# Grouped-query decode attention on one core: matmul addresses by bit masks, a three-pass y-sum for the last head, and an earlier row sum

## The chip, the cores and the metric

The kernel runs on one core of one Trainium2 chip. The metric is the device time of one execution in microseconds (us), taken in several runs on the same chip and given as a median. A profile of one execution gives busy times, waits and the records of single instructions and DMA packets; its span is about 2 us shorter than the device time. An execution counts as slow when it is over 1.5% above the fastest of its kernel; only fast ones are compared here, and where a kernel ran once its state is unknown. PE is the matrix engine, PEld its weight loads, PEq its sequencer, DVE the vector engine, ACT the scalar engine, POOL the general-purpose engine and SP the engine that issues the loads.

## The reference

One query token attends to 65536 keys. There are 32 query heads and 8 key/value heads, so four query heads share one head of K and V.

```python
B, Hq, Hkv, Sq, Sk, D = 1, 32, 8, 1, 65536, 128      # q, k, v: bf16
k = jnp.repeat(k, Hq // Hkv, axis=1)
v = jnp.repeat(v, Hq // Hkv, axis=1)
scores = jnp.einsum("bhqd,bhkd->bhqk", q, k) * D ** -0.5
out = jnp.einsum("bhqk,bhkd->bhqd", softmax(scores), v)
```

K and V are 134 MB each. Every byte is used once, for four heads.

## The kernel before

A head's keys are handled in two halves of 32768; each half fills a buffer of 128 partitions x 256 slots x 128 values (8 MB). There are two buffers for K and one for V. All loads go out from one queue in a fixed order, and each waits until PE is done with what stood in its buffer:

```python
def load_k(g, b):
    SP.wait((s_sc, 16 * g - 8 + 8 * b if g else 0))      # scores of the earlier head are done
    ...
def load_v(g, b):
    done = 2 * (2 * g + b)
    if (g, b) == (G - 1, 1):          # the last V load goes in eight pieces
        SP.wait((s_vc, done - 1))     # first half of the V buffer is free
        load(v, g, b, 0, s_v[0], CUTS[0], CUTS[1])
        SP.wait((s_vc, done))         # all of it is free
        ...
        for lo, hi, s in list(zip(CUTS, CUTS[1:], s_v))[1:]:
            load(v, g, b, 0, s, lo, hi)
    ... # two halves for the two V loads before that, else one load after s_vc >= done
# CUTS = [0, 128, 192, 224, 232, 240, 248, 252, 256], in slots
```

DVE transposes K in place, 64 or 128 slots at a time. PE then makes the scores. A half of K takes eight turns of a loop ("parts") of eight matmuls each; the addresses come from two counters, x (the tile) and n (the part):

```python
with block("pe_part"):
    nc.regs_alu(r_n, r_n, 1, op=ALU.add)
    ...                                     # x and n are the values of r_x and r_n
    r_k = (x % 2) * (SL * D) + (n // 2) * (PS * D) + (n % 2) * (2 * D) + SL * D
    r_w = (n % 4) * (-8) + 28
    r_o = (x % 2) * 1024 + (n // 4) * 512
    take(s_kt, 1)                           # wait for the transpose, count it down
    for u in range(2):
        for s in range(2):
            for e in range(2):
                i = pe.matmul(out=..r_o.., lhsT=..r_w.., rhs=..r_k.., ...)
    i.then_inc(s_sc, 1)
    nc.br_cmp(r_n, 7, "pe_part", "pe_skip", "IS_LT", engines=only)
```

The values of a half take 64 matmuls of 512 columns ("wide"), into four groups y of PSUM columns. Two spare matmuls in their middle write to a place that nobody reads for their value. After each head DVE multiplies by a selector and sums over the four y:

```python
def collect():
    n = DV.mark(dve.tensor_tensor(out=vy[:, :, :], in0=vacc,          # vy: [P, 4, D], fp32
        in1=sely[:, :, None].to_broadcast([P, 4, D]), op=ALU.mult))
    DV.after(n)
    return DV.mark(dve.tensor_reduce(out=vs[:, 0:D],
        in_=vy[:, :, :].rearrange("p y d -> p d y"), axis=AX.X, op=ALU.add))
```

For the last 24 slots, which arrive in small pieces, there are single narrow matmuls, with the row sum of the softmax among them. The last "gather" adds the y-sums; ACT scales, and a small store ends the program:

```python
for t in range(SL - TAIL, SL):
    if t == CUTS[5]:                        # slot 240
        pe.matmul(out=pl, lhsT=sel[:, :], rhs=vs[:, ...], start=True, stop=True).then_inc(s_pe, 1)
    if t in CUTS:
        pe.wait_ge(s_v[CUTS.index(t)], 16)  # this piece of V has landed
    pe.matmul(out=fin, lhsT=et[...], rhs=io[:, t, :], ...)
pe.wait_ge(s_dv, collected[G - 1])          # the y-sums are there
gather(D, start=False, stop=True).then_inc(s_pe, 1)
```

Of the kernel before, what the change touches and what calls it, by code (L numbers as in the profile page):

```python
# [8 lines left out]
ALU = mybir.AluOpType  # L9
ACT = mybir.ActivationFunctionType  # L10
AX = mybir.AxisListType
PE = mybir.EngineType.PE

P = 128
D = 128
SL = 256
KEYS = P * SL
G = 8
H = 4
WB = 160  # L20
PS = 64
TAIL = 24
CUTS = [0, 128, 192, 224, 232, 240, 248, 252, 256]
# [24 lines left out]
def kernel(  # L48
# [7 lines left out]
    nc = tc.nc  # L56
    SCALE = float(D) ** -0.5
    fp32 = mybir.dt.float32
# [5 lines left out]
    def sb(name, shape, dt):  # L64
        return ctx.enter_context(nc.sbuf_tensor(name, shape, dt))

    def ps(name, shape):
        return ctx.enter_context(nc.psum_tensor(name, shape, fp32))

    def sem(name):  # L70
        return ctx.enter_context(nc.semaphore(name))
# [7 lines left out]
    sel = sb("sel", [P, H], fp32)  # L79
    selq = sb("selq", [P, 16], fp32)  # L80
    sely = sb("sely", [P, 4], fp32)
# [5 lines left out]
    ex = sb("ex", [P, 4, 512], bf16)  # L87
    et = sb("et", [P, 2, 512], bf16)
    vs = sb("vs", [P, D + 2], fp32)
    vy = sb("vy", [P, 4, D], fp32)  # L90
    fall = sb("fall", [H, G - 1, D + 2], fp32)
    r7 = sb("r7", [H, G - 1], fp32)
    o = sb("o", [H, D], bf16)
# [2 lines left out]
    sc, vacc = acc[:, 0:2048], acc[:, 2048:2560].rearrange("p (y d) -> p y d", d=D)  # L96
    pt = ps("pt", [P, 512])
    pb = ps("pb", [P, 512])
    pf = ps("pf", [P, 512])
    pl, fin = pb[0:H, 8:9], pf[0:H, 0:D]  # L100
# [7 lines left out]
    s_sc, s_pe, s_vb, s_vc = sem("s_sc"), sem("s_pe"), sem("s_vb"), sem("s_vc")  # L108
# [11 lines left out]
    sp, act, dve, gp, pe = nc.sync, nc.scalar, nc.vector, nc.gpsimd, nc.tensor  # L120
    SP = Queue(nc, sp, None)
    ACTQ = Queue(nc, act, s_ac)
    DV = Queue(nc, dve, s_dv)
# [48 lines left out]
    for g in range(1, G):  # L172
# [11 lines left out]
    n = GP.mark(gp.memset(ident[:, :], 0.0))  # L184
    GP.after(n)
    p_ident = GP.mark(gp.affine_select(
        out=ident[:, :], in_=ident[:, :], compare_op=ALU.not_equal, fill=1.0, base=0,
        pattern=[[-1, P]], channel_multiplier=1,
    ))
    n = DV.mark(dve.memset(acc[:, :], 0.0))  # L190
    collected = {-2: n, -1: n}
# [3 lines left out]
        out=sel[:, :], in_=ident[:, :].rearrange("p (x h) -> p h x", h=H), axis=AX.X, op=ALU.add  # L195
    ))
    n = DV.mark(dve.tensor_reduce(
        out=selq[:, :], in_=ident[:, :].rearrange("p (x r) -> p r x", r=16), axis=AX.X, op=ALU.add
    ))
    DV.after(n)  # L200
    DV.mark(dve.tensor_reduce(
        out=sely[:, :], in_=selq[:, :].rearrange("p (y h) -> p y h", h=H), axis=AX.X, op=ALU.add
    ))
    DV.wait((s_q, 16))
    for a in range(4):
        d_qT = DV.mark(dve.transpose(
            out=qT[32 * a:32 * a + 32, :, :].rearrange("p s n -> p (s n)"),
            in_=q_in[:, :].bitcast(u32),
# [61 lines left out]
            in_=ex[:, 2 * b:2 * b + 2, :].rearrange("p i n -> p (i n)"),  # L270
        ).then_inc(s_et, 1)

    def collect():
        n = DV.mark(dve.tensor_tensor(  # L274
            out=vy[:, :, :], in0=vacc, in1=sely[:, :, None].to_broadcast([P, 4, D]), op=ALU.mult
        ))
        DV.after(n)
        return DV.mark(dve.tensor_reduce(  # L278
            out=vs[:, 0:D], in_=vy[:, :, :].rearrange("p y d -> p d y"), axis=AX.X, op=ALU.add
        ))  # L280

    def keep(g):
# [3 lines left out]
    for g in range(G):  # L286
        for _ in transposes(g, 0):
            pass
        for i, _ in enumerate(transposes(g, 1)):
            if i == 0 and g:  # L290
                DV.wait((s_vc, 4 * g - 2))
                weights(g - 1, 1)
        top(g)
        softmax(g)
        if 0 < g < G - 1:

            weights(g, 0)
            DV.wait((s_vc, 4 * g))
            collected[g - 1] = collect()
            ACTQ.wait((s_dv, collected[g - 1]))  # L300
            clear(g)
        elif g:
            DV.wait((s_vc, 4 * g))
            DV.after(collect())
            collected[g - 1] = DV.mark(dve.memset(vacc, 0.0))
            weights(g, 0)
        else:
            weights(g, 0)
        if g:
            n_kept = keep(g - 1)  # L310
# [4 lines left out]
    for i in range(2):  # L315
        n = DV.mark(dve.reciprocal(out=r7[:, i::2], in_=fall[:, i::2, D + i]))
    DV.after(n)
    n = DV.mark(dve.tensor_tensor(
        out=o7, in0=fall[:, :, 0:D], in1=r7[:, :, None].to_broadcast([H, G - 1, D]),
        op=ALU.mult,  # L320
    ))
    SP.wait((s_dv, n))
    sp.dma_start(
        out=out[0, 0:(G - 1) * H, 0, :].rearrange("(g h) d -> h g d", h=H), in_=o7
    ).then_inc(s_st, 16)
    DV.wait((s_vb, 2 * G))
    collected[G - 1] = collect()
    DV.wait((s_pe, 3 * G + 2))
    d_rl = DV.mark(dve.reciprocal(out=rl[:, :], in_=pl))
    ACTQ.wait((s_dv, d_rl), (s_pe, 3 * G + 3))  # L330
    n = ACTQ.mark(act.activation(out=o[:, :], in_=fin, func=ACT.Copy, scale=rl[:, :]))  # L331
# [5 lines left out]
    for g in range(G):  # L337
# [5 lines left out]
        for a in range(4):  # L343
            r = slice(32 * a, 32 * a + 32)
            c0 = 28 + 32 * a
            if a == 3:
# [4 lines left out]
                out=wz[r, :, c0:c0 + H].rearrange("p (s w) h -> p s w h", s=2),  # L351
                in_=qTb[r, :, :, g, :],
# [5 lines left out]
    def take(s, n):  # L358
        down(pe, PE, s, n, wait=True)
# [8 lines left out]
    def wide(ch, tt):  # L368
        c, w0 = tt % 4, tt * 32 + 16 * (ch % 2)
        return pe.matmul(  # L370
            out=vacc[32 * c:32 * c + 16, :, :],
            lhsT=et[:, ch // 2, w0:w0 + 16],
            rhs=io[:, PS * ch + 4 * tt:PS * ch + 4 * tt + 4, :],
            start=False, stop=False, skip_group_check=True,
        )

    only = OrderedEngineSet([PE])
    r_x, r_n = (nc.alloc_registers(r, engines=only) for r in ("x", "n"))

    def block(name):  # L380
        return nc.body(name, valid_engines=only)


    nc.regs_mov(r_x, -1)
    nc.br("pe_head", engines=only)
    with block("pe_head"):
        take(s_w, 4)
# [1 line left out]
        nc.br("pe_tile", engines=only)  # L389
    with block("pe_tile"):  # L390
        nc.regs_alu(r_x, r_x, 1, op=ALU.add)
        nc.regs_mov(r_n, -1)
        nc.br_cmp(r_x, 2 * G, "pe_part", "pe_skip", "IS_LT", engines=only)
    with block("pe_part"):
        nc.regs_alu(r_n, r_n, 1, op=ALU.add)
        x = nc.snap(r_x, engines=only, donate=True, min_val=0, max_val=2 * G + 1)
        n = nc.snap(r_n, engines=only, donate=True, min_val=0, max_val=7)
        r_k = (x % 2) * (SL * D) + (n // 2) * (PS * D) + (n % 2) * (2 * D) + SL * D
        r_w = (n % 4) * (-8) + 28
        r_o = (x % 2) * 1024 + (n // 4) * 512  # L400
        take(s_kt, 1)
        for u in range(2):
            for s in range(2):
                for e in range(2):
                    i = pe.matmul(  # L405
                        out=bass.AP(acc, r_o, [[2560, P], [1, 512]]),
                        lhsT=bass.AP(wz, r_w + ((2 * s + e) * WB - 4 * u), [[4 * WB, P], [1, P]]),
                        rhs=bass.AP(
                            io, r_k + (u * D + 64 * s + e), [[IO, P], [4 * D, 16], [2, 32]]
                        ),  # L410
                        start=False, stop=False, skip_group_check=True,
                    )
        i.then_inc(s_sc, 1)
        nc.br_cmp(r_n, 7, "pe_part", "pe_skip", "IS_LT", engines=only)
    with block("pe_skip"):
        nc.br_cmp(r_x, 2, "pe_next", "pe_values", "IS_LT", engines=only)
    with block("pe_values"):
        take(s_et, 1)
        for ch in range(4):
            if ch == 3:  # L420
                pe.wait_ge(s_v[2], 16)
            elif ch != 1:
                take(s_v[ch // 2], 16)
            for tt in range(16 if ch < 3 else (SL - TAIL) % PS // 4):
                if (ch, tt) == (3, 8):
                    pe.wait_ge(s_v[3], 16)
                i = wide(ch, tt)
            if ch == 1:
                i.then_inc(s_vc, 1)

                for _ in range(2):
                    pe.matmul(  # L432
                        out=pt[0:16, :], lhsT=et[:, 0, 0:16], rhs=et[:, 0, :],
                        start=True, stop=True,
                    )
        i.then_inc(s_vb, 1)
        nc.br_cmp(r_x, 2 * G + 1, "pe_rest", "pe_tail", "IS_LT", engines=only)
    with block("pe_rest"):
# [2 lines left out]
        i.then_inc(s_vc, 1)  # L441
        nc.br("pe_next", engines=only)
    with block("pe_next"):
        nc.regs_alu(r_n, r_x, 2, op=ALU.mod)
        nc.br_cmp(r_n, 0, "pe_tile", "pe_softmax", "IS_EQ", engines=only)
    with block("pe_softmax"):
        take(s_mg, 1)
# [3 lines left out]
            out=pb[:, 0:1], in_=nrow[:, :, :].rearrange("o x h -> o (x h)"), identity=ident[0:1, 0:1]  # L451
        ).then_inc(s_pe, 1)
        nc.br("pe_head", engines=only)
    nc.switch_bb("pe_tail")

    for t in range(SL - TAIL, SL):
        if t == CUTS[5]:
            pe.matmul(  # L458
                out=pl, lhsT=sel[:, :], rhs=vs[:, D + (G - 1) % 2:D + (G - 1) % 2 + 1],
                start=True, stop=True,  # L460
            ).then_inc(s_pe, 1)
        if t in CUTS:
            pe.wait_ge(s_v[CUTS.index(t)], 16)
        w0 = t % PS // 4 * 32 + 16 + 4 * (t % 4)
        pe.matmul(  # L465
            out=fin, lhsT=et[:, 1, w0:w0 + H], rhs=io[:, t, :], start=(t == SL - TAIL), stop=False,
            skip_group_check=True,
        )
# [32 lines left out]
```

## Time and profile before

| what | value | view |
|---|---|---|
| device time | 630.08 us, median of 3 (629.99 to 630.28) | runs |
| packets of the load queue | 99.1% of 16 DMA engines' span | queue table |
| PE, DVE, ACT busy | 56%, 54%, 6% | busy table |
| one part of the scores | 2.52 us, of which PE idles 0.6 us | timeline |
| last V piece landed to last gather | 0.30 us | semaphore records, timeline |

From the profile page of the kernel before, first the busy time of the engines (us, share of the span, number of instructions), then DMA by fortieths of the span (9 is 90% or more busy), then the load queue (packets, MB, share of 16 engines' span).

```profile
PE 352.5 (56%) x2136; PEld 138.0 (22%) x2136; DVE 339.2 (54%) x131; ACT 36.1 (6%) x32; POOL 7.5 (1%) x40
...
DMA  8999999999999999999999999999999999999996
...
q1 hardware_dynamic: 6656, 268.45, 99.1%
```

The load queue is the only thing that is busy all the time. No engine with arithmetic passes 56%.

From the groups of the same page (line, engine, operation, tiles out and in, number; then busy us and mean ns of one; then the idle time ahead of them and what ended it):

```profile
L405 PE MATMUL acc<-io,wz 128*128 x1024 | 270.7, 416 | 179.7 <-issue 92.2
L227 DVE STREAM_TRANSPOSE io<-io 128x4096 uint32<-128x4096 uint32 (+1 forms) x54 | 279.0, 5207 | 161.2 <-DMA io<-in_k_dram 161.2
...
L274 DVE TENSOR_TENSOR vy<-acc,sely 128x512 f32<-128x512 f32 x8 | 5.3, 660 | 11.9 <-PE acc L370 11.9
...
L278 DVE TENSOR_REDUCE vs<-vy 128x128 f32<-128x512 f32 x8 | 8.2, 1021 | 0.3
```

The score matmuls (L405) had 179.7 us of idle PE ahead of them, of which 92.2 us are labelled "issue": nothing that the profile shows was waited for. That label suggests register arithmetic, and the change aims at it. The timeline of PE in a K stage (start, duration, then in brackets the idle time ahead) shows it turn by turn:

```profile
44.98 1.91 PE L405 MATMUL acc<-io,wz 128*128 x8 [0.60 <-issue]
47.50 1.92 PE L405 MATMUL acc<-io,wz 128*128 x8 [0.61 <-issue]
50.07 1.92 PE L405 MATMUL acc<-io,wz 128*128 x8 [0.65 <-issue]
```

The timeline of the tail of the kernel before:

```profile
622.03 1.06 PE L370 MATMUL acc<-io,et 128*16 128x512 bf16 x10 [1.36 <-DMA io<-in_v_dram]
...
623.14 0.69 DVE L274 TENSOR_TENSOR vy<-acc,sely 128x512 f32<-128x512 f32 x1 [11.94 <-PE acc L370]
623.38 0.42 PEld L465 LDWEIGHTS pf<-io,et 128*4 128x4 bf16 x8 [0.59 <-DMA io<-in_v_dram]
...
623.83 0.19 PE L458 MATMUL pb<-vs,sel 128*4 128x1 f32 x2
623.86 1.03 DVE L278 TENSOR_REDUCE vs<-vy 128x128 f32<-128x512 f32 x1
624.04 0.87 PEld L465 LDWEIGHTS pf<-io,et 128*4 128x4 bf16 x16
...
624.95 0.09 PEld L364 LDWEIGHTS pf<-vs,sel 128*4 128x4 f32 x2
...
625.43 0.36 ACT L331 ACTIVATE o<-pf,rl 4x128 bf16<-4x128 f32 x1 [31.86 <-PE pf L364]
```

L465 are the single slots, L458 is the row sum, L278 the reduction, L364 the last gather. The pieces of V for slots 232, 240, 248 and 252 landed (last of 16 DMA engines, from the trace's semaphore records) at 623.34, 624.00, 624.34 and 624.65.

### The profile page before, as it was taken

The numbers are of one execution on the slowest core, as the hardware profiler recorded it, in microseconds if no ns is written. First come the engines' busy times: TensorE is split into PE (matmuls) and PEld (weight loads), VectorE is DVE, ScalarE is ACT, GpSimd is POOL, SyncE is SP. The second block draws the span as 40 slices with busy tenths as digits, with TensorE's granted clock in tenths as the row PEclk, the third lists the DMA queues.
The fourth block names the chain that finished last, engine by engine and source line by source line (L and its number), as shares of the span: only waits on it lengthen the run. The fifth ranks groups of instructions, "written<-read, shape, count | busy, mean of one in ns | idle before, by whom it ended". The sixth has DMA issues, their size and how long they took to land. (4 is left out here: it accounts for less than half of the span.)

```text
span 628.0 us, 6627 instructions
## 1 busy us (share of the span) xinstructions
PE 352.5 (56%) x2136; PEld 138.0 (22%) x2136; DVE 339.2 (54%) x131; ACT 36.1 (6%) x32; POOL 7.5 (1%) x40
## 2 busy tenths in 40 slices
PE   0676483834838348382573816748176581887335
PEld 0222131311313113130231302213022230332112
DVE  3984835649065490655807558085570846684211
ACT  0000200020000200002000020000200002000100
POOL 1000000000000000000000000000000000000000
PEclk9999596975969759596696966969669595899677
DMA  8999999999999999999999999999999999999996
GB/s 368 434 459 409 459 409 459 409 451 417 451 417 451 417 443 426 442 426 434 434 430 438 422 447 417 451 405 463 401 463 405 463 405 463 399 434 434 434 432 277
DMA packets 6715, 268.48 MB, mean 428 GB/s; under 512 B 825, under 2 KB 1081, under 8 KB 1465
## 3 DMA queue, kind: packets, MB, share of 16 engines
q1 hardware_dynamic: 6656, 268.45, 99.1%
q8 instruction: 1, 0.02, 0.0%
q10 hardware_dynamic: 56, 0.01, 0.0%
q14 instruction: 2, 0.01, 0.0%
HBM read 268.44 MB, written 0.01 MB: 427 GB/s over the span
## 5 line engine op out<-in xcount | busy, mean ns | idle before, releaser
L405 PE MATMUL acc<-io,wz 128*128 x1024 | 270.7, 416 | 179.7 <-issue 92.2
L227 DVE STREAM_TRANSPOSE io<-io 128x4096 uint32<-128x4096 uint32 (+1 forms) x54 | 279.0, 5207 | 161.2 <-DMA io<-in_k_dram 161.2
L405 PEld LDWEIGHTS acc<-io,wz 128*128 x1024 | 105.5, 103 | 345.0 <-issue 267.4
L370 PE MATMUL acc<-io,et 128*16 128x512 bf16 x1018 | 70.6, 409 | 22.3 <-PEq L113 20.9
L232 DVE TENSOR_REDUCE mg<-acc 128x1 f32<-128x2048 f32 x8 | 18.3, 2291 | 55.4 <-PE acc L405 55.4
L246 ACT ACTIVATE ex<-acc,nmb 128x2048 bf16<-128x2048 f32 x8 | 15.7, 1967 | 531.1 <-DVE nmb L244 531.1
L370 PEld LDWEIGHTS acc<-io,et 128*16 128x16 bf16 x1018 | 27.4, 94 | 61.1 <-issue 36.5
L364 PE MATMUL pf<-vs,sel 128*4 128x130 f32 (+1 forms) x20 | 5.7, 386 | 62.4 <-PEq L113 62.4
L268 DVE STREAM_TRANSPOSE et<-ex 128x1024 bf16<-128x1024 bf16 x16 | 19.6, 1225 | 30.0 <-PE acc L370 15.1
L257 ACT ACTIVATE acc<-wz 128x2560 f32<-128x2560 bf16 x7 | 16.1, 2307 | 17.7 <-DVE vs L278 17.6
L364 PEld LDWEIGHTS pf<-vs,sel 128*4 128x4 f32 x20 | 1.1, 83 | 62.8 <-issue 62.8
L236 DVE TENSOR_REDUCE m<-pt 1x4 f32<-1x128 f32 x8 | 2.2, 279 | 21.7 <-PE pt L448 21.7
L350 POOL COPY wz<-qT 32x16 bf16<-32x16 bf16 x32 | 6.1, 190 | 518.2 <-PE acc L405 434.5
L274 DVE TENSOR_TENSOR vy<-acc,sely 128x512 f32<-128x512 f32 x8 | 5.3, 660 | 11.9 <-PE acc L370 11.9
L432 PE MATMUL pt<-et 128*16 128x512 bf16 x32 | 10.0, 395 | 0.0
L278 DVE TENSOR_REDUCE vs<-vy 128x128 f32<-128x512 f32 x8 | 8.2, 1021 | 0.3
L450 PE MATMUL pb<-ident,nrow 1*128 1x1 f32 x8 | 1.6, 194 | 5.7 <-PEq L113 5.7
L432 PEld LDWEIGHTS pt<-et 128*16 128x16 bf16 x32 | 3.0, 94 | 4.4 <-issue 1.1
L448 PE MATMUL pt<-ident,mg 128*1 128x128 f32 x8 | 2.2, 270 | 2.5 <-PEq L113 2.5
L190 DVE MEMSET acc<- 128x2560 f32 x1 | 2.2, 2192 | 1.6 <-SPq L62 1.6
L244 DVE COPY nmb<-pb 128x1 f32<-128x1 f32 x8 | 1.3, 158 | 3.0 <-PE pb L450 3.0
L450 PEld LDWEIGHTS pb<-ident,nrow 1*128 1x128 f32 x8 | 1.1, 138 | 7.0 <-issue 7.0
(26 smaller groups left out, 16.0 us busy)
## 6 DMA issues: line engine op xcount, KB each, us to landing
io<-in_v_dram SPq DMA_DIRECT2D x5, 4096.0 KB, 16.5
io<-in_k_dram SPq DMA_DIRECT2D x4, 4096.0 KB, 25.9
io<-in_k_dram SPq DMA_DIRECT2D x4, 2048.0 KB, 39.8
io<-in_v_dram SPq DMA_DIRECT2D x1, 2048.0 KB, 10.7
io<-in_v_dram SPq DMA_DIRECT2D x1, 1024.0 KB, 12.8
io<-in_v_dram SPq DMA_DIRECT2D x3, 256.0 KB, 13.2
io<-in_v_dram SPq DMA_DIRECT2D x2, 128.0 KB, 13.2
io<-in_k_dram SPq DMA_DIRECT2D x13, 43.3
```

The lines of the kernel that those rows point to most:

```text
L227: dve.transpose(out=part, in_=part).then_inc(s_kt, n // 32)
L232: dve.tensor_reduce(out=mg[:, :], in_=sc, axis=AX.X, op=ALU.max).then_inc(s_mg, 1)
L246: n = ACTQ.mark(act.activation(out=ex[:, :, :].rearrange("p b n -> p (b n)"), in_=sc, func=ACT.Exp, bias=nmb[:, :], scale=SCALE, accum_out ...
L257: cleared[g] = ACTQ.mark(act.activation(out=acc[:, :], in_=wz[:, 0, 0:1].to_broadcast([P, 5 * 512]), func=ACT.Copy))
L268: dve.transpose(out=et[:, :, :].rearrange("p i n -> p (i n)"), in_=ex[:, 2 * b:2 * b + 2, :].rearrange("p i n -> p (i n)"),).then_inc(s_et, 1)
L274: n = DV.mark(dve.tensor_tensor(out=vy[:, :, :], in0=vacc, in1=sely[:, :, None].to_broadcast([P, 4, D]), op=ALU.mult))
L278: return DV.mark(dve.tensor_reduce(out=vs[:, 0:D], in_=vy[:, :, :].rearrange("p y d -> p d y"), axis=AX.X, op=ALU.add))
L350: gp.tensor_copy(out=wz[r, :, c0:c0 + H].rearrange("p (s w) h -> p s w h", s=2), in_=qTb[r, :, :, g, :],).then_inc(s_w, 1)
L364: return pe.matmul(out=pf[0:H, 0:w], lhsT=sel[:, :], rhs=vs[:, 0:w], skip_group_check=True, **kw)
L370: return pe.matmul(out=vacc[32 * c:32 * c + 16, :, :], lhsT=et[:, ch // 2, w0:w0 + 16], rhs=io[:, PS * ch + 4 * tt:PS * ch + 4 * tt + 4, : ...
L405: i = pe.matmul(out=bass.AP(acc, r_o, [[2560, P], [1, 512]]), lhsT=bass.AP(wz, r_w + ((2 * s + e) * WB - 4 * u), [[4 * WB, P], [1, P]]), r ...
L432: pe.matmul(out=pt[0:16, :], lhsT=et[:, 0, 0:16], rhs=et[:, 0, :], start=True, stop=True,)
```

## The change

Its intent is to shorten the register work between parts, to drop one of the two spare matmuls, to make the y-sum of the last head faster, and to take the row sum out of the last singles. The diff, cut to its core:

```diff
-    vy = sb("vy", [P, 4, D], fp32)
+    vy = sb("vy", [P, D, 4], fp32)
+    vz = ...                       # the same memory as [P, 4, D]
-    def collect():
+    def collect(last=False):
-            out=vy[:, :, :], in0=vacc, ...
+            out=vy[:, :, :].rearrange("p d y -> p y d") if not last else vz, in0=vacc, ...
-            out=vs[:, 0:D], in_=vy[:, :, :].rearrange("p y d -> p d y"), axis=AX.X, op=ALU.add
+        if not last:
+            ... out=vs[:, 0:D], in_=vy[:, :, :], axis=AX.X, op=ALU.add
+        n = DV.mark(dve.tensor_tensor(
+            out=vz[:, 0:2, :], in0=vz[:, 0:2, :], in1=vz[:, 2:4, :], op=ALU.add))
+        DV.after(n)
+        return DV.mark(dve.tensor_tensor(
+            out=vs[:, 0:D], in0=vz[:, 0, :], in1=vz[:, 1, :], op=ALU.add))
...
+    r_q_bits = {nc.alloc_registers(f"q{b}", engines=only): b for b in (8, 112, 24, 96)}
...
-        nc.regs_alu(r_n, r_n, 1, op=ALU.add)
-        r_k = (x % 2) * (SL * D) + (n // 2) * (PS * D) + (n % 2) * (2 * D) + SL * D
-        r_w = (n % 4) * (-8) + 28
-        r_o = (x % 2) * 1024 + (n // 4) * 512
+        nc.regs_alu(r_q, r_q, 8, op=ALU.add)
+        for r, bits in r_q_bits.items():
+            nc.regs_alu(r, r_q, bits, op=ALU.bitwise_and)
+        r_k = n8 * (2 * D // 8) + m8 * (PS * D // 16) + SL * D
+        r_w = w8 * (-1) + 28
+        r_o = o8 * 16
...
-        nc.br_cmp(r_n, 7, "pe_part", "pe_skip", "IS_LT", engines=only)
+        nc.regs_alu(r_n, r_q, 56, op=ALU.bitwise_and)
+        nc.br_cmp(r_n, 56, "pe_part", "pe_skip", "IS_LT", engines=only)
...
-                for _ in range(2):
-                    pe.matmul(out=pt[0:16, :], ...)          # spare
+                pe.matmul(out=pt[0:16, :], ...)              # spare
...
-        nc.regs_alu(r_n, r_x, 2, op=ALU.mod)
+        nc.regs_alu(r_n, r_x, 1, op=ALU.bitwise_and)
...
+    pe.matmul(out=pl, lhsT=sel[:, :], rhs=vs[:, ...], ...).then_inc(s_pe, 1)
     for t in range(SL - TAIL, SL):
-        if t == CUTS[5]:
-            pe.matmul(out=pl, lhsT=sel[:, :], rhs=vs[:, ...], ...).then_inc(s_pe, 1)
```

## The prediction

> **What bounds the kernel.** The loads of K and V. The page's queue table has 268.45 MB on one queue, whose packets take 99.1% of 16 engines' span; the stretches table has the engines' share at 0.98 to 1.06 and 426 to 459 GB/s in every stretch from 5 to 600 us. [...]268.45 MB in the 622 us from first to last packet are 431 GB/s[...]. PE is 56% busy, DVE 54%. Loads are never short of a free buffer: a 4 MB V load, 9.7 us at this rate, lands 16.5 us after its issue, so about 7 us of queue stand ahead of it.
>
> **What the change does.**
> 1. Address arithmetic. In the K stage the timeline shows one part of eight matmuls every 2.52 us: 1.91 busy, 0.61 idle "issue", so registers cost up to 0.6 us a part. The masks should remove most of it: an estimate of 2.0 to 2.3 us a part where DVE is ahead. 128 parts x 0.3 us are some 40 us of PE time, all off the chain: PE then waits for transposes (4.38 us for two parts) or for K. Worth 0.
> 2. One spare matmul instead of two per value tile: 16 x 0.4 us of PE time. The next load goes earlier into a full queue. Worth 0.
> 3. The strided product and the reduction in the other heads: DVE has slack. Worth 0. I expect the reduction (1.02 us, reading at a stride) to get shorter, perhaps 0.7 us, the product unchanged at 0.66.
> 4. The tail. The chain of waits has 13.25 us of V transfer up to 623.3, then single slots, the last gather (624.95), scaling (625.43) and store. On DVE the last product ends at 623.83 and the reduction takes 1.03 us. [...]
> 5. The row sum ahead of the singles takes 0.2 us of PE from between the singles to before 623.34, where PE waits for V anyway. But the second group of singles starts at 624.04 because its V piece lands at 624.00, not because of the row sum; the last piece lands at 624.65, its four singles start at 624.69, and the last is issued by about 624.87. So the gather can start no earlier than 624.87, against 624.95: of the 0.5 us removed, 0.08 us is on the chain.
>
> **Prediction.** 630.0 us, 629.4 to 630.6 in 8 of 10 cases; faster by over 2%: 0.005, within 2%: 0.99, slower by over 2%: 0.005.
>
> **What would show it right.** The queue share stays near 99% and the rate near 428 GB/s. PE's idle "issue" before the score matmuls and its period per part drop, while DVE's idle time waiting for K stays near 161 us. In the tail: [...]row sum before the singles; the second group still starts where its piece lands; the gather starts 0.22 to 0.25 us after the last landing, where it was 0.30.
>
> **What would make it wrong.** A load rate drifting by 0.1% is 0.6 us, more than the gain. Stragglers among the 16 engines at the end may hide the 0.08 us[...]. If parts do not get shorter, the masks were not what filled the gap; the time would still stand.

The forecast's sum is 630.08 us, measured for the kernel before, less the 0.08 us of step 5, so 630.0 us; steps 1 to 3 count 0. The 0.08 us is read from the trace, but holds only if the y-sums are ready by 624.87 us (before: 624.89); that they would be was the author's estimate. The "0.5 us removed" of step 5 still counts the cut gain on DVE beside the row sum's 0.2 us.

## The result, and the profile after

The kernel with the change took 630.23 us (median of 6 runs, 629.81 to 630.38); the kernel before took 630.23 us in its 6 runs. The ratio is 0.9997, with a 95% interval of 0.9984 to 1.001. Ratios here are the mean time of one kernel's fast runs over that of the other's of the same rounds, so not quite the ratio of the medians quoted.

The busy times and the load queue of the kernel after, from its page:

```profile
PE 346.7 (55%) x2120; PEld 136.0 (22%) x2120; DVE 339.2 (54%) x132; ACT 36.1 (6%) x32; POOL 7.5 (1%) x40
...
q1 hardware_dynamic: 6656, 268.45, 99.1%
```

PE lost 6 us of busy time. Sixteen spare matmuls fewer account for some 3.5 us of it (an estimate: 16 x 0.22 us; the median from the start of one score matmul, of as many columns, to the next within a part is 219 ns in the trace before and 218 in the one after). The 40 us that the prediction gave to the masks were idle time and have to be looked for in the gaps. The queue is as full as it was. The groups of the same page:

```profile
L422 PE MATMUL acc<-io,wz 128*128 x1024 | 268.5, 413 | 184.3 <-PEq L114 180.6
...
L275 DVE TENSOR_TENSOR vy<-acc,sely 128x512 f32<-128x512 f32 x8 | 7.8, 980 | 12.0 <-PE acc L380 12.0
...
L281 DVE TENSOR_REDUCE vs<-vy 128x128 f32<-128x512 f32 x7 | 4.8, 686 | 0.2
```

Here is a trap. The label "issue", 92.2 us before, has all but gone: the 180.6 us are now put down to PEq L114, a helper's line that here takes the transposes' semaphore. But the idle time as a whole did not fall (179.7 us before, 184.3 after). The total alone would prove nothing, since saved time turns into waiting for loads (it is 191.5 us in the last experiment below, where the gap is gone). What counts is that the gap of each turn is as long as it was, as the timeline of the kernel after shows:

```profile
49.70 1.90 PE L422 MATMUL acc<-io,wz 128*128 x8 [0.68 <-PEq L114]
52.23 1.90 PE L422 MATMUL acc<-io,wz 128*128 x8 [0.63 <-PEq L114]
54.82 1.91 PE L422 MATMUL acc<-io,wz 128*128 x8 [0.68 <-PEq L114]
```

The median time from part to part, worked out from the matmul records, is 2.53 us before and 2.58 after. Only the name of the gap changed. The records of the PE sequencer say why. These are the instructions between two parts, in one turn of each kernel, with the start of each counted from the first one and its duration, both in ns:

```
before                                after
COMPARE_BRANCH    0, 207              ALU_OP (mask 56)    0,  36
ALU_OP (n + 1)  266,  36              COMPARE_BRANCH     97, 207
EVENT_SEMAPHORE 402,  51              ALU_OP (q + 8)    363,  36
FUSED_REGOPS    553, 211              ALU_OP (mask)     459,  36
FUSED_REGOPS    822, 206              ALU_OP (mask)     556,  32
FUSED_REGOPS   1086, 167              ALU_OP (mask)     649,  32
FUSED_REGOPS   1311,  65              ALU_OP (mask)     741,  32
first weights  1426                   EVENT_SEMAPHORE   834,  51
                                      FUSED_REGOPS     1024, 143
                                      FUSED_REGOPS     1225,  74
                                      ALU_OP           1358,  36
                                      first weights    1422
```

The divisions had been fused: three instructions of about 0.2 us each, and a short one, did all of the address work. Now two fused ones are gone and a third is shorter, but six single register instructions have come. All but the last take 92 to 97 ns from the start to that of the next instruction (36 ns or less by their own record). Both sequences take about 1.4 us: over the 94 turns of each trace that took less than 2.75 us, the median from the first instruction to the first weights is 1396 ns before and 1422 after.

The tail of the kernel after, from its timeline:

```profile
622.20 1.06 PE L380 MATMUL acc<-io,et 128*16 128x512 bf16 x10 [1.38 <-DMA io<-in_v_dram]
...
623.14 0.38 PE L471 MATMUL pb<-vs,sel 128*4 128x1 f32 x2
623.30 0.69 DVE L275 TENSOR_TENSOR vy<-acc,sely 128x512 f32<-128x512 f32 x1 [11.96 <-PE acc L380]
623.56 0.42 PEld L479 LDWEIGHTS pf<-io,et 128*4 128x4 bf16 x8 [0.33 <-DMA io<-in_v_dram]
...
624.03 0.42 DVE L284 TENSOR_TENSOR vy<-vy 128x256 f32<-128x256 f32 x1
624.19 0.87 PEld L479 LDWEIGHTS pf<-io,et 128*4 128x4 bf16 x16 [0.21 <-DMA io<-in_v_dram]
624.49 0.29 DVE L288 TENSOR_TENSOR vs<-vy 128x128 f32<-128x128 f32 x1
...
625.03 0.14 PEld L374 LDWEIGHTS pf<-vs,sel 128*4 128x4 f32 x2
...
625.57 0.36 ACT L341 ACTIVATE o<-pf,rl 4x128 bf16<-4x128 f32 x1 [31.61 <-PE pf L374]
```

The four pieces landed at 623.51, 624.15, 624.49 and 624.81. The two sums take 0.42 and 0.29 us in place of 1.03; the row sum is done before the singles; the second group of singles starts 0.04 us after the piece for slot 240 landed, as it did before; and the gather starts 0.22 us after the last landing, against 0.30. The gain of 0.08 us is there in the trace, one execution each, but the last piece itself landed 0.16 us later in this execution than in the one before, and no run-to-run comparison sees either.

### The profile page after: what moved, and what is told of

Same layout as the page of the kernel before. It is cut to its first block, busy times and chain, and to the rows that moved or that the text cites. A ratio compares the mean times of both kernels' runs of the same rounds, so it can differ in the third digit from the quotient of the medians.

```text
span 628.1 us, 7091 instructions
## 1 busy us (share of the span) xinstructions
PE 346.7 (55%) x2120; PEld 136.0 (22%) x2120; DVE 339.2 (54%) x132; ACT 36.1 (6%) x32; POOL 7.5 (1%) x40
## 3 DMA queue, kind: packets, MB, share of 16 engines
q1 hardware_dynamic: 6656, 268.45, 99.1%
## 5 line engine op out<-in xcount | busy, mean ns | idle before, releaser
L422 PE MATMUL acc<-io,wz 128*128 x1024 | 268.5, 413 | 184.3 <-PEq L114 180.6
L380 PE MATMUL acc<-io,et 128*16 128x512 bf16 x1018 | 67.8, 409 | 23.6 <-PEq L114 22.2
L275 DVE TENSOR_TENSOR vy<-acc,sely 128x512 f32<-128x512 f32 x8 | 7.8, 980 | 12.0 <-PE acc L380 12.0
L449 PE MATMUL pt<-et 128*16 128x512 bf16 x16 | 6.3, 395 | 0.0
L281 DVE TENSOR_REDUCE vs<-vy 128x128 f32<-128x512 f32 x7 | 4.8, 686 | 0.2
L294 ACT ACTIVATE fall<-pf 4x130 f32<-4x130 f32 x7 | 1.9, 269 | 7.5 <-PE pf L374 7.5
```

Of the source, the lines that this page charges most:

```text
L275: n = DV.mark(dve.tensor_tensor(out=vy[:, :, :].rearrange("p d y -> p y d") if not last else vz, in0=vacc, in1=sely[:, :, None].to_broadca ...
L281: return DV.mark(dve.tensor_reduce(out=vs[:, 0:D], in_=vy[:, :, :], axis=AX.X, op=ALU.add))
L380: return pe.matmul(out=vacc[32 * c:32 * c + 16, :, :], lhsT=et[:, ch // 2, w0:w0 + 16], rhs=io[:, PS * ch + 4 * tt:PS * ch + 4 * tt + 4, : ...
L422: i = pe.matmul(out=bass.AP(acc, r_o, [[2560, P], [1, 512]]), lhsT=bass.AP(wz, r_w + ((2 * s + e) * WB - 4 * u), [[4 * WB, P], [1, P]]), r ...
L449: pe.matmul(out=pt[0:16, :], lhsT=et[:, 0, 0:16], rhs=et[:, 0, :], start=True, stop=True)
```

## The experiments

Theory A is that the loads alone set the time, so that PE and DVE work off the tail is worth nothing while the loads keep ahead. Rival B is that the arithmetic counts, and that the change gained nothing because one of its parts failed. The trace speaks for a mixture: the masks did fail. So both were tried.

### Loads alone

All arithmetic is taken out. The same pieces are loaded in the same order on the same queue; each load waits only for the earlier load into its buffer, and the last two V loads go to the K buffers, so that no load waits for one that was issued just ahead of it. The result is wrong on purpose.

```diff
-    ... all of DVE, ACT, POOL and PE
+    for key in SEQ:                                  # the order of the kernel before
+        SP.wait((own[at], count[at]))                # the earlier load into this buffer
+        for lo, hi in zip(cuts, cuts[1:]):
+            load(k if w == "k" else v, g, b, at, own[at], lo, hi)
+    for s, n in zip(own, count):
+        act.wait_ge(s, n)
+    act.dma_start(out=out[0, :, 0, :], in_=io[0:G * H, 2 * SL, :]).then_inc(s_st, 16)
```

> No arithmetic at all: the same loads in the same pieces on the same queue, each waiting only for the earlier load into its buffer, then one small store (result wrong on purpose). Theory A (the loads alone set the time): the loads end near 624 us as before, and the whole takes 626 to 629 us, less than the kernel before only by the arithmetic between the last landing and the store, about 1 to 2 us. Rival B (the arithmetic slows the loads, or holds their buffers): clearly shorter, below 620 us.

Measured: 627.87 us (4 runs, 627.78 to 628.27) beside 630.21 us of the kernel before; ratio 0.9962 (0.9946 to 0.9979). Its queue table:

```profile
q1 hardware_dynamic: 6624, 268.44, 99.4%
```

All of the arithmetic costs 2.3 us of 630 (1.3 to 3.4 by the interval). No change to PE or DVE can gain more than that, 0.4%, while the loads stay as they are. Nor does the arithmetic slow the transfers: a 64 KiB packet has a median of 2.42 us and a mean of 2.424 us in this kernel, in the one before and in the one after.

### More work for PE

The changed kernel gets spare matmuls in front of the last wide matmuls of a V tile, which delays the release of the V buffer, in 15 of the 16 tiles (not in the last). One costs some 0.22 us, as above; with ten more the trace has 380.8 us of PE busy time, 34.1 more than that of the kernel after, which is 0.23 us for each of the 150.

```diff
     with block("pe_rest"):
+        for _ in range(10):                          # 40 in the other run
+            pe.matmul(out=pt[0:16, :], lhsT=et[:, 0, 0:16], rhs=et[:, 0, :], start=True, stop=True)
```

> The changed kernel with ten more spare matmuls ahead of the release of each value buffer, 15 times, 2 to 4 us each, 30 to 60 us of PE time in all. Theory A: some 7 us of queue stand ahead of each V load, so nothing shows: within 0.2% of the kernel before. Rival B (PE time counts): 660 us or more.

> The same with forty spare matmuls, 9 to 17 us each time. Theory A: this exceeds the queue of about 7 us ahead of each V load, the queue runs dry, and the time rises by 15 times the excess: 30 to 150 us longer. Were nothing to show here either, the slack would be larger than I read it.

Measured: 637.94 us with ten (636.04 to 638.30; ratio 1.0113) and 673.53 us with forty (672.48 to 674.18; ratio 1.0682). The second is as theory A has it in size, though the queue did not run dry 15 times: the six second halves of heads 0 to 5 cost 5 to 6 us each, the last head some 9 us, the other loads next to nothing. The first is a miss: 150 spares, 34 us of PE busy time, cost 8 us, not 0. It contradicts the prediction's "about 7 us of queue", so that number was worked out anew from the DMA packets: the lead of a load is the time from its issue to the (median) end of the last 16 packets of the loads issued before it.

| kernel | lead of the V loads, second half of heads 0 to 5 | lead of the V loads, first half of heads 1 to 6 |
|---|---|---|
| before | 3.2 to 4.0 us | 7.9 to 8.0 us |
| after | 4.1 to 5.1 us | 8.4 to 9.7 us |
| after, ten more spares | 0.5 to 2.0 us | 6.0 to 6.3 us |
| after, forty more spares | -4.6 to -3.7 us | 5.7 to 6.0 us |

The lead was half of what I had read. The 16.5 us from issue to landing less 9.7 us of transfer came from the five half-size V loads at the end, of which some stand far better than the full-size ones. And a lead has to be more than 0: the first packet comes 1.0 us after the issue (333.37 to 334.33 us in the run with ten, 0.95 to 1.99 us for the first load of the kernel before). In the run with ten, fewer than ten of the 16 DMA engines were busy for 0.33 us at 334.1 and for 0.79 us at 412.5, and most of the first packets after such a gap took 2.6 to 3.4 us in place of 2.42. Between the first and the last packet, the run with ten lost 3.5 us to longer packets and 3.3 us to idle engines against the kernel after; 1.2 us more came behind the last packet. That is the difference of the spans, 8.0 us. Not all of it belongs to the short leads: 1.3 us of the idle time lie at the very end, where some engines lagged. The last piece of V landed from the first engine at 628.47 us, from the fifteenth at 630.37 and from the sixteenth at 631.58 (623.80, 624.13 and 624.81 in the kernel after). Why they lagged stays open. The queue's share says how often it ran dry, first with ten, then with forty:

```profile
q1 hardware_dynamic: 6656, 268.45, 98.4%
```

```profile
q1 hardware_dynamic: 6656, 268.45, 93.4%
```

So theory A holds with a limit: the lead of the second halves, 3 to 4 us before the change, less the 1.0 us from issue to first packet, is about what can be spent, not 7 us. The edge is not sharp: at the leads of 2.0, 1.6 and 1.2 us of heads 0 to 2 the run with ten already fell another 0.4, 0.4 and 0.7 us behind the kernel after. And the change did one useful thing that no time shows: in these two executions it widened the leads by 0.5 to 1.5 us.

### Half loads: what the change is worth when PE sets the time

From head 1 on, only the first half of each load is fetched; waits and arithmetic stay. The result is wrong, since stale slots are used again.

```diff
     def load(src, g, b, at, s, lo=0, hi=SL):
+        if g:
+            hi = lo + (hi - lo) // 2
```

This was put into the kernel before, into the kernel before with the masks alone, and into the whole change. A fourth kernel is the whole change with two parts in one turn of the loop; the odd part uses constant offsets.

```diff
-        nc.regs_alu(r_q, r_q, 8, op=ALU.add)
+        nc.regs_alu(r_q, r_q, 16, op=ALU.add)
...
-        take(s_kt, 1)
-        for u in range(2): ...
+        for odd in range(2):
+            take(s_kt, 1)
+            for u in range(2): ...               # lhsT offset - 8 * odd, rhs offset + 2 * D * odd
+            i.then_inc(s_sc, 1)
```

> The kernel before with only the first half of each load from head 1 on (result wrong on purpose, all waits and arithmetic as they were), so that about 350 us of loads stand beside at least 450 us of PE work. A base for the next three; by the theory that PE then sets the time, 470 to 530 us.

> The same with only the address masks of the change. Prediction's step 1 (the masks shorten a part by 0.3 us or so): 38 us shorter than half_before. Rival, from the traces (a part went from 2.53 to 2.58 us: five register instructions cost what the fused ones with divisions did): the same to 7 us longer.

> The whole change under half loads. Sixteen spare matmuls fewer, 0.2 to 0.43 us each: 3 to 7 us shorter than half_masks. By the rival on the masks this is 0 to 7 us shorter than half_before; by the prediction's step 1, 40 us or more.

> The whole change under half loads, with two parts per turn of the loop, the odd one by constant offsets: the same matmuls and fused operations, half the turns. If the number of register and branch instructions ahead of each part's first matmul fills the gap, half of it goes and the transposes of 4.4 us for two parts take over: a pair in 4.4 to 4.6 us instead of 5.1, 30 to 45 us shorter than half_after. If the gap is something else (a latency of weights or of PSUM), no change.

| kernel, half loads | median us (range) | median part to part, us |
|---|---|---|
| before | 528.59 (528.30 to 530.34) | 2.53 |
| masks alone | 526.09 (525.22 to 528.42) | 2.58 |
| whole change | 523.65 (521.59 to 524.80) | 2.58 |
| whole change, two parts a turn | 464.96 (463.90 to 466.62) | 1.75 |

The masks are worth 2.5 us, not 38, where PE is the limit: step 1 of the prediction falls. (They lengthen a part by 0.05 us, so 2.5 us to the good are themselves unexplained; the profiled executions of the two kernels had the same span, 526.3 us. I leave that open.) The rest of the change brings another 2.4 us, a little less than the expected 3 to 7. Halving the turns brings 58.7 us, more than expected. The timelines of PE, first half loads with the whole change, then with two parts a turn:

```profile
300.42 1.90 PE L424 MATMUL acc<-io,wz 128*128 x8 [0.68 <-PEq L114]
302.95 1.90 PE L424 MATMUL acc<-io,wz 128*128 x8 [0.64 <-PEq L114]
```

```profile
295.95 12.25 PE L425 MATMUL acc<-io,wz 128*128 x48 [5.66 <-PEq L114]
```

The gap of 0.65 us is gone altogether, since 1.75 us a part is eight matmuls at 0.22 us. The matmuls are the same, and nearly so are the fused operations (17 for two parts in place of 18), so what filled the gap is the sequencer's run of instructions per turn, about 1.4 us. That run comes half as often here; it is also somewhat shorter, about 1.2 us, with one mask fewer. That sixteen matmuls in flight hide it where eight do not is how I read it; the runs show only that the gap goes.

### The tail without its last landings

The last three pieces of the last V load (slots 240 to 255) are not fetched; their semaphores are raised at once. The piece for slot 232 is then the last to land, and no later landing can hide what the tail costs. The result is wrong on purpose. It was put into the kernel before, into the kernel with one of the two tail parts, and into the whole change; one profiled execution each, the state unknown.

```diff
             for lo, hi, s in list(zip(CUTS, CUTS[1:], s_v))[1:]:
-                load(v, g, b, 0, s, lo, hi)
+                if lo < 240:
+                    load(v, g, b, 0, s, lo, hi)
+                else:
+                    sp.sem_inc(s, 16)
```

> The kernel before without the last three pieces of the last V load (slots 240 to 255; result wrong on purpose): the piece of slots 232 to 239 lands last, so no later landing can hide the tail's work. From that landing to the last gather: 1.6 us (singles and row sum on PE, and the reduction on DVE, both end then).

> The same with only the three passes of the y-sum. DVE is ready 0.3 us earlier, but PE still has the row sum between its singles: gather 1.55 to 1.6 us after the landing, so 0 to 0.05 us of gain.

> The same with only the row sum ahead of the singles. PE is done 0.27 us earlier, but waits for the reduction: gather still 1.6 us after the landing.

> Both parts: gather 1.3 us after the landing, 0.3 us gained, where neither part alone gains. With the last landings in place the traces show only some 0.08 us (gather 0.30 us after the last landing before, 0.22 after).

| kernel | last landing to gather | PE clock granted from 622 to 624 us (1.00 is full speed) |
|---|---|---|
| before | 623.38 to 625.72: 2.34 us | 0.52 |
| three passes alone | 623.28 to 624.66: 1.38 us | 1.00 |
| row sum ahead alone | 623.14 to 624.79: 1.65 us | 1.00 |
| both | 623.35 to 625.14: 1.79 us | 0.63 |

Two of the four executions had a granted PE clock of 0.52 and 0.63 there, so only the two middle rows can be compared; the experiment does not measure the 0.3 us of both parts, which stays open. The middle rows do tell something, and against my expectation. The lines of PE weights and DVE from the timeline with the three passes alone:

```profile
623.33 0.42 PEld L478 LDWEIGHTS pf<-io,et 128*4 128x4 bf16 x8 [0.53 <-DMA io<-in_v_dram]
...
623.72 0.14 PEld L471 LDWEIGHTS pb<-vs,sel 128*4 128x4 f32 x2
...
623.80 0.89 PEld L478 LDWEIGHTS pf<-io,et 128*4 128x4 bf16 x16
...
624.32 0.29 DVE L291 TENSOR_TENSOR vs<-vy 128x128 f32<-128x128 f32 x1
...
624.66 0.14 PEld L377 LDWEIGHTS pf<-vs,sel 128*4 128x4 f32 x2
```

and with the row sum ahead alone:

```profile
624.79 0.09 PEld L367 LDWEIGHTS pf<-vs,sel 128*4 128x4 f32 x2 [0.29 <-DVE vs L281]
```

The row sum takes 0.08 us out of the middle of the singles, from 623.72 to 623.80, not the 0.2 to 0.27 us that I had put down to it (in the kernel before, most of that gap was the wait for slot 240). With the row sum ahead alone, PE idles 0.29 us for the reduction. So the y-sum is the part that matters once landings do not hide it, 0.27 us between these two rows (one execution each), and the row sum hardly does: with the three passes alone the y-sum is ready at 624.61 and the gather starts at 624.66, so taking the row sum away as well could gain 0.05 us at most there.

### Two parts a turn, whole loads

The kernel with two parts a turn is correct, so it was run with its full loads as a candidate to beat both.

> The two-parts-per-turn loop, which took 59 us off the kernel under half loads, with the whole loads: a correct kernel with a real saving on PE. Theory A (the loads alone set the time): 629.5 to 630.8 us, ratio to before 0.998 to 1.001; a part in about 1.75 to 2.2 us instead of 2.5; the loads are issued further ahead of the end of the queue (narrowest lead from some 4 to some 5 us or more). Were the masks' missing saving the reason that the change gained nothing, this one would be shorter by several us.

Measured: 630.35 us (5 runs, 630.01 to 630.64) beside 630.16 us; ratio 0.9995 (0.9981 to 1.0009). What took 59 us off with half loads takes nothing off here. The group of DVE transposes in its profile shows where the time went:

```profile
L228 DVE STREAM_TRANSPOSE io<-io 128x4096 uint32<-128x4096 uint32 (+1 forms) x54 | 279.0, 5207 | 182.7 <-DMA io<-in_k_dram 182.7
```

DVE waits 182.7 us for K to arrive, where it was 161.2 us before: the saved time turned into waiting for loads. The leads of the second halves of heads 1 to 5 grew to 6.9 to 8.0 us (those of the last head's first four V loads stayed at 4.1 to 5.9, where they were 4.4 to 5.3 before). It has more room, but it is not faster.

## Why the prediction was right or wrong

- **The time**: predicted 630.0 us (629.4 to 630.6), measured 630.23. Right, and for the main reason given: the loads bound the kernel. The run with loads alone (627.87 us) and the one with two parts a turn (630.35 us, in spite of 59 us saved under half loads) show that directly.
- **Step 1, the masks**: wrong. "The masks should remove most of it" did not happen: 2.53 us a part became 2.58, and the masks brought 2.5 us under half loads, where about 38 had been expected. The idle time labelled "issue" did drop from 92.2 to 1.3 us, which the prediction named as a sign of being right; the label only moved to the semaphore instruction that now stands next to the gap. What failed is the premise, an estimate that no trace had shown, that cheaper arithmetic shortens the gap: the gap comes with the whole run of sequencer instructions in a turn, and the masks replaced a few long ones by more short ones. From the first of them to the first weights the median is 1396 ns before and 1422 after.
- **Step 2, the spare matmul**: right that it is worth nothing here; 2.4 us (together with the rest of the change, not separated) under half loads.
- **"About 7 us of queue"**: wrong by a factor of two. The narrowest lead was 3.2 to 4.0 us. The conclusion survived since the change made the lead larger, which is luck as far as the number goes; the number misled the expectation of the first experiment on PE work, which missed by 8 us.
- **Step 3, the other heads**: half right. The reduction fell from 1019 to 686 ns, near the guess of 0.7 us (medians 1019 before; all of the seven after at 686 or 687). The product did not stay at 0.66 us: writing at a stride of four elements, it went from a median of 652 to 1016 ns. The two cancel: 1671 ns before, 1702 after. One of the two works at a stride in either layout. Three contiguous passes would take 652 + 425 + 291 = 1368 ns, an estimate from the trace; it was not run for the other heads, whose y-sum is off the chain.
- **Step 4, the three passes**: right that they are shorter than the reduction: 425 and 291 ns in the trace after, where the last head's reduction took 1032 in the one before.
- **Step 5, the tail's chain**: right in what bounds it. The second group of singles started where its piece landed, and the gather came 0.22 us after the last landing (predicted 0.22 to 0.25, before 0.30). The size given to the row sum, 0.2 us of PE, was wrong; the tail run with the three passes alone shows 0.08 us.

## What to carry to other kernels

Before pricing a saving on an engine, find out how long the kernel takes without any arithmetic, and how far the narrowest load is issued ahead of the end of its queue; the first bounds every gain (2.3 us here), the second says how much more work is free (less than 3 us per V tile here). Judge a gap by its length from turn to turn, not by the label that the profile puts on it: here 92.2 us of the label became 1.3, and the time from part to part did not fall (2.53 and 2.58 us). In a loop on the sequencer, count instructions per turn and do more work in each turn before rewriting the arithmetic of an address: under half loads two parts a turn took off 58.7 us, the masks 2.5.

## What the traces show besides

- In both traces the record of the branch that ends a part on PE's sequencer is 207 to 227 ns in the 112 of 128 turns that jump back, with the next instruction 266 ns after its start in the turns printed above, and 76 to 79 ns in the 16 that leave the loop.
- Of the register instructions on PE's sequencer, a simple one takes 32 to 36 ns by its record but, in the turns printed above, 92 to 97 ns from start to start; a fused one takes 65 to 243 ns by its record (trace before). The 7 (before) or 11 (after) instructions between two parts, branch and semaphore included, make 1.4 us (medians of 1396 and 1422 ns).
- On DVE a 512-element fp32 product written at a stride of four elements took a median of 1016 ns, against 652 contiguous. A 512-element reduction read at a stride of 128 elements took 1019 ns, against 686 contiguous. Why a stride costs that much these runs do not show.
- With this one core streaming, 268.45 MB in the 622 us from first to last packet are 431 GB/s.
- With ten more spares, the first packets of 64 KiB after a gap in the load queue took up to 3.4 us in place of 2.42, and with leads of 0.5 to 2.0 us the span was 8.0 us longer, though not all of that belongs to the leads.
